# One kernel, five engine programs: the instruction order of attention, gated MLP and expert mixture written out as a table

## The chip, the core and the metric

The kernel runs on one core of a Trainium2 chip. A core has five engines with an instruction stream each: TensorE (PE in the profile; PEld is its loading of weights), VectorE (DVE), ScalarE (ACT), GpSimd (POOL) and SyncE (SP), which here only issues DMA transfers. Engines run beside each other and wait on semaphores for one another; within a stream, instructions start in the order in which they stand there. The metric is the device time of one execution in microseconds (us), as the median of several runs.

## The reference

Three stages, one after the other:

```python
# attention, 4 batches x 8 heads, 576 tokens, 64 wide; 32 landmarks = means of 18 tokens
A, Bm, C = sm(q, k_lm), sm(q_lm, k_lm), sm(q_lm, k)
Z = Bm.T / (norm1(Bm) * norminf(Bm) + 1e-6)
for _ in range(6): Z = 2 * Z - Z @ Bm @ Z
x = A @ Z @ C @ v                                   # -> 2304 tokens x 512
# gated MLP, 512 -> 1536 -> 512
xn = x / sqrt(mean(x * x) + 1e-6) * rms_g
x = (silu(xn @ w_gate) * (xn @ w_val)) @ w_out
# mixture: tokens with x @ w_skip > 0 add gate * relu(x @ w1[e]) @ w2[e], e = argmax(x @ w_gate2)
```

The three MLP weights arrive as 64-bit floats and are turned into 32-bit ones on the chip, by shifts and scaled copies on their bit patterns.

## The kernel before, in words

**Stages.** Attention works per batch in two groups of four heads (`group`): landmarks of k and q, three score matrices, then the iterated inverse (`inverse`). Its result is not formed in full: per batch a small matrix `WT` remains, and `products` multiplies it into the weights (P = WT x weight, kept as a high and a low half, `rsplit`). The MLP then runs in eight units of 288 tokens (`run_unit`): for each of 12 blocks `gemm` gives `pg` and `pv`, ACT takes a tanh of `pg` (tile `h`) and casts the product to `h_t`, POOL subtracts to get the low half, and `project` sums over all 12 blocks into `o`, which goes to `x2T`. `finish` stores x2T, makes the logits (`lp`) and transposes x2T for the output. Two calls of `mixture` follow, and a loop for more expert/batch pairs.

**Weights.** `load_raw` loads a piece of w_gate or w_val (256 rows by 512 columns of 64-bit floats, 1 MB, tile `wr`, three buffers that it shares with q and k of batch 0); `convert_w` turns it into tile `wo` by four operations (DVE scales into `s64`, ACT makes two partial copies into `wo`, DVE combines) and stores it to a scratch tensor in HBM (`wg_d`, `wv_d`) for later batches. Twelve pieces are treated so, five of them beside the attention of batch 0 and the rest during unit 0. `load_wout` and `convert_wout` do the same for twelve pieces of w_out.

**What sets the order.** The program is emitted once, in Python; generators in the list `side` are advanced between the matmuls of the main line by `slot()`, which goes by rough sums of busy time that `Paced` keeps per engine (`PER`, `FIXED`, `SLACK`). The framework's scheduler then orders each engine's stream from the emission order and its dependencies. Every operation of PE, DVE, ACT and POOL goes through `Paced.__getattr__`, so all of them carry line L62 in the profile. SP's transfers keep their own lines: L230 loads q and k, L254 v, L771 raw gate/value weights, L781 stores converted ones, L789 loads w_out, L812 loads converted weights again, L949 stores results, L1255 loads the scale `gcol`.

In the rows, `plm` are the landmark sums, `pb`, `sq`, `sk` scores, `nr`/`nu` the matmuls of the inverse, `X` and `Rb` its running matrices, `blk` its last X spread on a block diagonal, `pG`, `Gbd` and `oT` what follows, `asum`, `arec`, `sT`, `AT` the softmax of the first score matrix and its transposition.

Of the kernel before, what the change touches and what calls it, by code (L numbers as in the profile page):

```python
# [35 lines left out]
NC0 = 5  # L36
SLACK = 700


class Paced:  # L40

# [3 lines left out]

    def __init__(self, eng, busy, name):
        self.eng, self.busy, self.name = eng, busy, name

    def __getattr__(self, op):
        f = getattr(self.eng, op)  # L50

        def call(*args, **kw):
            size = max(math.prod(a.shape[1:]) for a in args[:3] if hasattr(a, "shape"))
            if self.name == "P":
                a = args[1] if op == "transpose" else args[2]
                size = math.prod(a.shape[1:])
                if op == "matmul" and a.dtype == F32:
                    size *= 4
                    if args[1].shape[0] == D:
                        size /= 2  # L60
            self.busy[self.name] += self.FIXED[self.name] + size * self.PER[self.name]
            return f(*args, **kw)  # L62

        return call


def attention_moe_kernel(
    tc, q, k, v, w_gate, w_val, w_out, rms_g, w_skip, w_gate2, w1, w2, out
):
    nc = tc.nc  # L70
    busy = dict.fromkeys("VAGP", 0.0)
    V, A, G, PE = (
        Paced(e, busy, n)
        for e, n in (
            (nc.vector, "V"), (nc.scalar, "A"), (nc.gpsimd, "G"), (nc.tensor, "P")
        )
    )
    SP = nc.sync
    ctx = ExitStack()

    def pool(stack, name, bufs=1, **kw):
        return stack.enter_context(tc.tile_pool(name=name, bufs=bufs, **kw))
# [36 lines left out]
    at = pool(pha, "at", side="right")  # L119
# [93 lines left out]
    def wo_tile(dt):  # L213
        return big.tile([128, 2, DM], dt, name="wo", tag="wo", bufs=FC)
# [10 lines left out]
    def load_qk(b, hg, n, t=None):  # L225
        if t is None:
            t = raw.tile([128, J, D], F32, name="kq")
        else:
            t = t.rearrange("p (j d) -> p j d", d=D)
        SP.dma_start(  # L230
            t.rearrange("p j d -> p (j d)"),
# [13 lines left out]
    def load_v(b, h0):  # L245
# [7 lines left out]
        for t in range(3):  # L253
            SP.dma_start(  # L254
                vt[32 * t : 32 * t + 32].rearrange("l h c d -> l h (c d)"), vv[t]
# [505 lines left out]
    def parts_at(d, i):  # L761
        n, g, q = PARTS[i]
        w = d.shape[1] // NQ
        return d[256 * g : 256 * g + 256, w * q : w * q + w].rearrange(
            "(c p) n -> p c n", p=128
        )

    def load_raw(i):
        if i < len(PARTS) and i not in raws:
            r = st1.tile([128, 2, J * D], I32, name="wr", tag="raw")[:, :, 0 : 2 * DM]  # L770
            SP.dma_start(r, parts_at(wsrc[PARTS[i][0]].bitcast(I32), i))  # L771
            raws[i] = r.rearrange("p c (n t) -> p c n t", t=2)

    def convert_w(i):
# [4 lines left out]
        for a in (1, 2):  # L779
            load_raw(i + a)  # L780
        SP.dma_start(parts_at(w_d[PARTS[i][0]], i), w)  # L781
        wparts[PARTS[i]] = w
# [3 lines left out]
    def load_wout(f):  # L786

        r = wo_tile(I32).rearrange("p a n -> p (a n)")
        SP.dma_start(r, w_out.bitcast(I32)[128 * f : 128 * f + 128, :])  # L789
        wo_raw.append(r.rearrange("p (n t) -> p n t", t=2))  # L790
# [9 lines left out]
    def load_w(n, q, last=False):  # L800

        ws = []
        for c in range(2):
# [7 lines left out]
            for g in range(2):  # L811
                SP.dma_start(  # L812
                    w[64 * g : 64 * g + 64],
# [221 lines left out]
    def ld(lst, idx, mx):  # L1035
        return nc.values_load(
            lst[0:1, bass.ds(idx, 1)], engines=(SPE,), min_val=0, max_val=mx
        )

    def number(lst):  # L1040
        return nc.values_load(lst[0:1, 2 * LP : 2 * LP + 1], min_val=0, max_val=B * E)

    def pair_at(lst, i):
        return ld(lst, i, E - 1), ld(lst, i + LP, B - 1)
# [166 lines left out]
    def drain(g):  # L1211
        for _ in g:
            pass
        if g in side:
            side.remove(g)
# [3 lines left out]
    def run_unit(u, before):  # L1219
# [32 lines left out]
        fin.append(finish(u, x2T))  # L1252
        side.insert(0, fin[0])

    SP.dma_start(gcol, rms_g.rearrange("(g c p) -> p g c", p=128, g=2))  # L1255

    def first_convs():
# [136 lines left out]
    for _ in mixture(*first["pair"], after_first, False):  # L1394
        next(oth, None)
        next(oth, None)
    drain(mixture(*second[0], lambda: pair_at(rest[0], 1), True, rest[1]))
    npairs = number(rest[0])
    with tc.For_i(0, npairs) as i:
        e, b = pair_at(rest[0], i + 1)  # L1400
# [36 lines left out]
```

## Time and profile before

| | |
|---|---|
| median of 3 runs | 673.87 us (672.52 to 674.31) |
| profiled execution, its own time | 678.17 us |
| span of its instructions | 676.4 us |
| busy: PE, DVE, ACT, POOL | 632.3, 434.9, 275.8, 146.4 us |
| instructions: PE, DVE, ACT, POOL | 4963, 997, 593, 162 |
| HBM read, written | 76.97 MB, 19.34 MB |

The span is the time from the first to the last instruction; 1.77 us of the profiled execution lie around it. PE is busy for 93% of the span, but not evenly: the busy tenths in 40 slices of 16.9 us begin 5, 7, 6, 7, 9, 8, 8 and stand at 9 nearly throughout after the tenth slice. The same part of the line PEclk (the granted clock of TensorE in tenths of full speed) reads 8, 9, 7, 7, 8, 8, 8. So the first 130 us are the part in which PE waits and runs below full speed. A time beside a matmul is what it took in its place; at a lower granted clock the same matmul takes longer.

### The profile page before, as it was taken

The page shows a single profiled execution, that of the slowest core. Times are in us where ns is not written, and L with a number is a line of the kernel's source. Part 1 is how long each engine was busy: PE and PEld are TensorE (multiplying, and loading weights), DVE is VectorE, ACT ScalarE, POOL GpSimd, SP SyncE. Part 2 cuts the span into 40 slices and gives each one's busy share as a digit, 9 for nine tenths or more (in the row PEclk, how much of TensorE's full clock was granted, in tenths as well). Part 3 has the DMA queues.
Part 4 walks back from the last instruction along what each step waited for, and adds up shares of the span by engine and source line. Part 5 has one row for each costly group of instructions (what it writes and reads, how often), then busy time and mean ns, then how long its engine had stood idle before and what let it go on. Part 6 is the DMA issues. An engine that isn't in the chain of part 4 may idle for free.

```text
span 676.4 us, 13386 instructions
## 1 busy us (share of the span) xinstructions
PE 632.3 (93%) x4963; PEld 548.9 (81%) x4963; DVE 434.9 (64%) x997; ACT 275.8 (41%) x593; POOL 146.4 (22%) x162
## 2 busy tenths in 40 slices
PE   5767988889998999999999999999999999999997
PEld 5653558877976888979889978999999988988985
DVE  6877778779769678896759966451645354353351
ACT  2358878534125422432531444240533343243240
POOL 5000234214101400410320320140552033033030
PEclk8977888999999999999999999999999999999999
DMA  8557779443248444249453316501644564364463
GB/s 274 216 215 251 261 264 336 117 107 87 71 104 215 93 110 106 67 126 194 87 110 87 75 45 147 126 8 27 178 127 100 165 206 140 123 174 146 141 181 137
DMA packets 111566, 97.16 MB, mean 144 GB/s; under 512 B 50192, under 2 KB 92176, under 8 KB 111504
## 3 DMA queue, kind: packets, MB, share of 16 engines
q1 hardware_dynamic: 111504, 96.34, 50.5%
q8 instruction: 38, 0.62, 0.4%
q14 instruction: 24, 0.20, 0.1%
HBM read 76.97 MB, written 19.34 MB: 142 GB/s over the span
## 4 chain that ended last, share of the span: by engine, by line
PE 74%; DVE 12%; DMA 6%; ACT 4%; issue 2%; POOL 1%; SPq 1%; POOLq 0%; DVEq 0%; ACTq 0%
PE o L62 18%; PE py L62 12%; PE ph L62 11%; PE pv L62 10%; PE pg L62 8%; PE P L62 4%; PE sq L62 3%; DMA wo<-in_moe_w_out_dram 2%; PE nr L62 2%; DMA wr<-wv_d 2%; DMA kq<-in_q_dram 2%; ACT wo L62 1%; DVE h L62 1%; DVE P L62 1%; PE sk L62 1%
## 5 line engine op out<-in xcount | busy, mean ns | idle before, releaser
L62 PE MATMUL o<-h_t,wo 128*128 128x288 f32 x1152 | 166.4, 300 | 3.6 <-ACT wo L62 1.8
L62 PEld LDWEIGHTS o<-h_t,wo 128*128 128x128 f32 x1152 | 156.0, 190 | 10.9 <-issue 5.1
L62 POOL TENSOR_TENSOR h_t<-h,h_t 128x288 fp32r<-128x288 f32 x96 | 83.8, 875 | 340.6 <-ACT h_t L62 274.7
L62 PE MATMUL pg<-ap_t,P 128*128 128x288 f32 x576 | 99.6, 303 | 7.9 <-DVE h L62 3.1
L62 PE MATMUL pv<-ap_t,P 128*128 128x288 f32 x576 | 99.5, 302 | 3.2 <-DVE P L62 1.6
L62 PEld LDWEIGHTS pg<-ap_t,P 128*128 128x128 f32 x576 | 82.8, 189 | 21.3 <-issue 9.3
L62 PEld LDWEIGHTS pv<-ap_t,P 128*128 128x128 f32 x576 | 83.0, 189 | 8.9 <-issue 2.7
L62 PE MATMUL ph<-xsh,P 128*128 128x288 f32 x384 | 77.6, 295 | 0.0
L62 PEld LDWEIGHTS ph<-xsh,P 128*128 128x128 f32 x384 | 61.9, 188 | 0.3
L62 DVE SCALAR_TENSOR_TENSOR h<-h,pg 128x288 f32<-128x288 f32 x96 | 42.6, 447 | 28.6 <-ACT h L62 28.1
L62 ACT CAST h_t<-h 128x288 fp32r<-128x288 f32 x96 | 41.1, 430 | 41.5 <-DVE h L62 41.4
L62 PE MATMUL ph<-xsl,P 128*128 128x288 f32 x192 | 56.8, 296 | 0.0
L62 ACT ACTIVATE h<-pg 128x288 f32<-128x288 f32 x96 | 39.2, 409 | 42.5 <-PE pg L62 37.9
L62 PE MATMUL py<-wo,h_t 128*128 128x512 f32 x210 | 51.4, 395 | 0.0
L62 PEld LDWEIGHTS py<-wo,h_t 128*128 128x128 f32 x210 | 39.4, 188 | 9.6
L62 DVE TENSOR_TENSOR h<-h,pv 128x288 f32<-128x288 f32 x96 | 42.8, 450 | 5.9 <-PE pv L62 1.8
L62 DVE STREAM_TRANSPOSE T<-kq 64x576 f32<-64x576 f32 (+1 forms) x40 | 35.4, 886 | 5.9 <-DMA kq<-in_k_dram 4.1
L62 ACT CAST P<-P 128x512 fp32r<-128x512 f32 x48 | 26.1, 586 | 31.2 <-PE P L62 30.6
L62 DVE TENSOR_TENSOR P<-P,P 128x512 fp32r<-128x512 f32 x48 | 31.4, 684 | 9.3 <-ACT P L62 9.2
L62 POOL TENSOR_TENSOR P<-w1r,P 128x512 fp32r<-128x512 f32 x16 | 21.0, 1315 | 72.3 <-ACT P L62 72.2
L62 PEld LDWEIGHTS ph<-xsl,P 128*128 128x128 f32 x192 | 36.0, 188 | 0.1
L62 DVE SCALAR_TENSOR_TENSOR h_t<-ph,h_t 128x288 fp32r<-128x288 f32 (+2 forms) x45 | 14.6, 353 | 27.6 <-ACT h_t L62 27.6
(222 smaller groups left out, 864.2 us busy)
## 6 DMA issues: line engine op xcount, KB each, us to landing
wl<-wg_d SPq DMA_DIRECT2D x36, 256.0 KB, 4.7
wr<-wv_d SPq DMA_DIRECT2D x32, 256.0 KB, 5.4
w1r<-in_moe_w_dram SPq DMA_DIRECT2D x32, 256.0 KB, 3.2
wr<-in_moe_w_gate_dram SPq DMA_DIRECT2D x6, 1024.0 KB, 6.7
wr<-in_moe_w_val_dram SPq DMA_DIRECT2D x6, 1024.0 KB, 6.6
wo<-in_moe_w_out_dram SPq DMA_DIRECT2D x12, 512.0 KB, 6.6
wo<-in_moe_w_dram SPq DMA_DIRECT2D x24, 256.0 KB, 5.1
kq<-in_k_dram SPq DMA_DIRECT2D x8, 576.0 KB, 4.1
```

The lines of the kernel that those rows point to most:

```text
L62: return f(*args, **kw)
```

## The change

A table `ORDER` is added: five lists, for PE, DVE, ACT, POOL and SP, each of pairs (skip, count) that walk through the instructions of that engine in the order in which they were emitted and so name a new order. `Paced` records every instruction it emits in `traced`, and a class `Queue` does so for SP's transfers. `arrange()`, called once behind the second mixture and before the loop, ties each instruction of an engine to the one that the table puts ahead of it, by an edge that only fixes their order. Nothing is computed otherwise: the instructions on each engine are the same ones, in the same number, on the same tiles. The table's order was found by list scheduling with durations taken from traces.

```diff
+ORDER = [
+    [int(x) for x in s.split()]
+    for s in (
+        "0 9 2 9 -11 2 9 4 4 5 -8 3 -4 1 8 4 2 5 -7 1 6 16 -22 1 21 7 4 1 -4 3 -4 1 4 3 1 "
...
+    )
+]
@@ class Paced
+        self.traced = []
...
         def call(*args, **kw):
+            ins = f(*args, **kw)
+            self.traced.append(ins.ins)
...
-            return f(*args, **kw)
+            return ins
@@
+class Queue:
+    def __init__(self, eng):
+        self.eng, self.traced = eng, []
+
+    def dma_start(self, *args, **kw):
+        ins = self.eng.dma_start(*args, **kw)
+        self.traced.append(ins.ins)
+        return ins
@@ def attention_moe_kernel
-    SP = nc.sync
+    SP = Queue(nc.sync)
@@
+    def arrange():
+        info = mybir.DependencyInfo(
+            mybir.DependencyClass.NoSync, mybir.DependencyReason.DATA
+        )
+        for eng, runs in zip((PE, V, A, G, SP), ORDER):
+            at, last = 0, None
+            for skip, n in zip(runs[0::2], runs[1::2]):
+                at += skip
+                for ins in eng.traced[at : at + n]:
+                    if last is not None:
+                        tc.add_manual_dep(ins, last.name, info, reason="order")
+                    last = ins
+                at += n
@@
     drain(mixture(*second[0], lambda: pair_at(rest[0], 1), True, rest[1]))
+    arrange()
```

In the changed kernel the recorded operations carry L160 and SP's transfers L183.

**The start.** On PE, before, the landmark sums of the second group (`plm_200`) stand on both sides of the small score matmul `pb`:

```order
L62 MATMUL plm_166<-kq_138,ident_94 128x128 x9
L62 MATMUL plm_200<-kq_141,ident_94 128x128 x5
L62 MATMUL pb_192<-lmk0_165,bdq_190 128x32 x2
L62 MATMUL plm_200<-kq_141,ident_94 128x128 x4
L62 MATMUL sq_215<-T_162,bdq_190 128x288 x2
```

and now:

```order
L160 MATMUL plm_166<-kq_138,ident_94 128x128 x9
L160 MATMUL plm_200<-kq_141,ident_94 128x128 x9
L160 MATMUL pb_192<-lmk0_165,bdq_190 128x32 x2
L160 MATMUL sq_215<-T_162,bdq_190 128x288 x2
L160 MATMUL sq_218<-T_162,bdq_190 128x288 x2
```

The last four of the second group's sums have moved ahead of `pb`, and the scores `sq` follow it at once. On SP the load of `gcol` has moved from the first place to the thirteenth, behind q, k and the first weights.

**The end of batch 0's attention.** On DVE, before, from the fourth step of the second group's inverse to the matrices that follow it (`s64` and `wo` are weight conversions):

```order
L62 TENSOR_TENSOR X_567<-nu_563,X_532 128x32
L62 SCALAR_TENSOR_TENSOR wo_311<-s64_312,wo_311 128x1024
L62 TENSOR_REDUCE asum_520<-sT_505 128x18
L62 TENSOR_TENSOR X_575<-nu_571,X_567 128x32
L62 TENSOR_SCALAR asum_520<-asum_520 128x18
L62 RECIPROCAL arec_523<-asum_520 128x18
L62 TENSOR_TENSOR X_583<-nu_579,X_575 128x32
L62 TENSOR_TENSOR sT_505<-sT_505,arec_523 128x576
L62 TENSOR_SCALAR s64_346<-wr_275 128x1024
L62 STREAM_TRANSPOSE AT_133<-sT_505 128x576
L62 TENSOR_TENSOR X_587<-nu_585,X_583 128x32
L62 TENSOR_TENSOR blk_589<-X_587,mask_105 128x128
```

and now:

```order
L160 TENSOR_TENSOR X_567<-nu_563,X_532 128x32
L160 SCALAR_TENSOR_TENSOR wo_311<-s64_312,wo_311 128x1024
L160 TENSOR_TENSOR X_575<-nu_571,X_567 128x32
L160 RECIPROCAL crec_465<-csum_463 128x1
L160 TENSOR_SCALAR mrn_295<-mask_105,rn_289 128x4
L160 TENSOR_SCALAR mrn_495<-mask_105,rn_489 128x4
L160 TENSOR_TENSOR X_583<-nu_579,X_575 128x32
L160 TENSOR_TENSOR X_587<-nu_585,X_583 128x32
L160 TENSOR_TENSOR blk_589<-X_587,mask_105 128x128
L160 TENSOR_SCALAR s64_346<-wr_275 128x1024
L160 TENSOR_TENSOR Gbd_594<-pG_591,mrn_295 128x256
L160 TENSOR_REDUCE asum_520<-sT_505 128x18
```

The softmax sum, its division, the transposition to `AT` and one conversion have left the place between `X_567` and `blk_589`; they stand behind `blk_589` now, and three small operations have come in.

**Unit 0.** On ACT, before, the partial copies of weight conversions (`wo`) alternate with the unit's own work (`h` the tanh, `h_t` its cast, `P0`, `P1` casts of products):

```order
L62 ACT_TABLE_LOAD
L62 ACTIVATE h_727<-pg_720 128x288
L62 ACTIVATE h_747<-pg_740 128x288
L62 ACTIVATE wo_818<-wr_776 128x1024
L62 CAST h_t_679<-h_727 128x288
L62 ACTIVATE wo_847<-wr_815 128x1024
L62 CAST h_t_679<-h_747 128x288
L62 ACTIVATE h_767<-pg_760 128x288
L62 ACTIVATE wo_847<-wr_815 128x1024
L62 ACTIVATE h_796<-pg_789 128x288
```

and now:

```order
L160 ACT_TABLE_LOAD
L160 ACTIVATE h_727<-pg_720 128x288
L160 ACTIVATE h_747<-pg_740 128x288
L160 ACTIVATE wo_847<-wr_815 128x1024 x2
L160 CAST P1_675<-P_827 128x512
L160 ACTIVATE wo_896<-wr_824 128x1024 x2
L160 ACTIVATE wo_945<-wr_853 128x1024 x2
L160 CAST h_t_679<-h_727 128x288
L160 ACTIVATE h_767<-pg_760 128x288
```

Six partial copies now stand between the second and the third tanh, and the cast of the first block has moved behind them. On SP, before, each load of a raw weight stands behind a store of a converted one:

```order
L771 DMA wr_776<-in_moe_w_val_dram 128x2x1024
L781 DMA wg_d_58<-wo_770 128x2x512
L771 DMA wr_815<-in_moe_w_gate_dram 128x2x1024
L781 DMA wv_d_59<-wo_809 128x2x512
L771 DMA wr_824<-in_moe_w_gate_dram 128x2x1024
L781 DMA wv_d_59<-wo_818 128x2x512
L771 DMA wr_853<-in_moe_w_val_dram 128x2x1024
L781 DMA wg_d_58<-wo_847 128x2x512
```

and now:

```order
L183 DMA wr_776<-in_moe_w_val_dram 128x2x1024
L183 DMA wg_d_58<-wo_391 128x2x512
L183 DMA wr_815<-in_moe_w_gate_dram 128x2x1024
L183 DMA wg_d_58<-wo_770 128x2x512
L183 DMA wr_824<-in_moe_w_gate_dram 128x2x1024
L183 DMA wv_d_59<-wo_809 128x2x512
L183 DMA wr_853<-in_moe_w_val_dram 128x2x1024
L183 DMA wv_d_59<-wo_818 128x2x512
```

Every load has moved ahead of one store: `wr_815` stood behind the store of `wo_770` and now stands before it, and so for the next ones.

Further on, the transposition of a unit's result for the output (`x2`) has moved from between the two DVE evacuations of `o` to some 20 places behind them, later products stand earlier in the `o` matmuls at the end of a unit, and loads of converted weights stand ahead of result stores on SP. In the two mixtures PE's order is unchanged.

## Rows read from the trace of the kernel before

**Rows 1.** Busy time by stage: window, us, busy (count) per engine, PEclk, DMA share, GB/s.

```profile
0.00:59.00 59.00, 40.12 (x272) 31.97 (x272) 41.67 (x131) 27.41 (x52) 8.64 (x26) 0.86 0.66 230
59.00:104.80 45.80, 40.52 (x198) 24.72 (x199) 36.89 (x62) 36.66 (x61) 11.17 (x10) 0.89 0.80 281
104.80:132.00 27.20, 22.34 (x150) 21.11 (x148) 22.36 (x36) 20.18 (x35) 10.62 (x9) 0.94 0.68 206
132.00:213.00 81.00, 74.31 (x642) 62.75 (x643) 64.26 (x149) 27.48 (x69) 12.20 (x14) 1.00 0.45 113
213.00:500.00 287.00, 283.47 (x2651) 253.34 (x2652) 194.14 (x472) 107.96 (x267) 69.98 (x80) 1.00 0.44 104
500.00:676.40 176.40, 171.57 (x1057) 155.03 (x1056) 75.60 (x151) 56.13 (x111) 33.76 (x25) 1.00 0.49 149
```

**Rows 2.** PE at the start: start us, us, engine, line, operation, tiles [idle before].

```profile
13.02 0.74 PE L62 MATMUL pb<-lmk,bdq 128*128 128x32 f32 x4 [1.91 <-DVE bdq L62]
13.57 2.06 PE L62 MATMUL plm<-kq,ident 128*128 128x128 f32 x8
15.42 1.17 PE L62 MATMUL sq<-T,bdq 128*128 128x288 f32 x2
```

**Rows 3.** SP at the start: the issue of the first load.

```profile
0.80 0.45 SPq L1255 DMA_DIRECT2D gcol<-in_moe_rms_g_dram  x1
```

**Rows 4.** DVE at the end of batch 0's attention.

```profile
41.48 0.19 DVE L62 TENSOR_TENSOR X<-nu,X 128x32 f32<-128x32 f32 x1 [1.30 <-PE nu L62]
41.76 1.23 DVE L62 SCALAR_TENSOR_TENSOR wo<-s,wo 128x1024 int32<-128x1024 int32 x1
42.90 0.75 DVE L62 TENSOR_REDUCE asum<-sT 128x18 f32<-128x576 f32 x1
43.56 0.18 DVE L62 TENSOR_TENSOR X<-nu,X 128x32 f32<-128x32 f32 x1
...
44.47 0.19 DVE L62 TENSOR_TENSOR X<-nu,X 128x32 f32<-128x32 f32 x1 [0.32 <-PE nu L62]
44.58 0.75 DVE L62 TENSOR_TENSOR sT<-sT,arec 128x576 f32<-128x576 f32 x1
45.24 0.69 DVE L62 TENSOR_SCALAR s<-wr 128x1024 f32<-128x1024 f32 x1
45.85 0.77 DVE L62 STREAM_TRANSPOSE AT<-sT 128x576 f32<-128x576 f32 x1
...
46.73 0.29 DVE L62 TENSOR_TENSOR blk<-X,mask 128x128 f32<-128x128 f32 x1
```

**Rows 5.** ACT in the same stretch: two partial copies of a conversion.

```profile
43.58 2.52 ACT L62 ACTIVATE wo<-wr 128x1024 int32<-128x1024 uint16 x2
```

**Rows 6.** SP's longest waits on stores of converted weights: total, times, longest us.

```profile
SPq L781 <- DVE wo L62: 48.7, 8, 17.7
```

**Rows 7.** From the chain of waits, unit 0: start us, us, what.

```profile
101.36 11.65 DMA wo<-in_moe_w_out_dram
```

**Rows 8.** PE, first matmuls of unit 1.

```profile
131.95 1.07 PE L62 MATMUL pg<-ap_t,P 128*128 128x288 f32 x6 [1.59 <-DVE x2T L62]
```

**Rows 9.** DVE in the w_out conversions: one operation twice.

```profile
107.68 1.57 DVE L62 TENSOR_TENSOR wo<-wf,wo 128x512 fp32r<-128x512 f32 x1 [1.54 <-ACT wo L62]
...
112.64 0.69 DVE L62 TENSOR_TENSOR wo<-wf,wo 128x512 fp32r<-128x512 f32 x1
```

**Rows 10.** POOL beside the first of the two.

```profile
107.44 1.26 POOL L62 TENSOR_TENSOR wo<-wf,wo 128x512 fp32r<-128x512 f32 x1
```

**Rows 11.** Busy time by window at the end of batch 0's attention, columns as above.

```profile
40.00:60.00 20.00, 13.01 (x52) 9.39 (x52) 12.39 (x25) 13.92 (x22) 0.00 (x0) 0.66 0.80 263
```

**Rows 12.** PE: products of WT and a weight, in two places.

```profile
61.59 3.42 PE L62 MATMUL P<-wo,WT 128*64 128x512 f32 x8
...
78.21 1.93 PE L62 MATMUL P<-wo,WT 128*64 128x512 f32 x6
```

99 rows, old and new, of the table ORDER are left out of this document.

## The prediction

> **What bounds the kernel now.** I read the profile from coarse to fine. First the table of busy time by stage [rows 1]. There the reader is to compare PE's busy time with the length of each stretch, and to read the granted clock beside it. From 213 us on PE is busy for 283.47 of 287.00 us and 171.57 of 176.40 us at a clock of 1.00: 3.5 and 4.8 us of idle in 463 us. Up to 213 us it is idle for 59.00 - 40.12 = 18.9, 45.80 - 40.52 = 5.3, 27.20 - 22.34 = 4.9 and 81.00 - 74.31 = 6.7 us, 35.8 us in all, and the clock stands at 0.86, 0.89 and 0.94 in the first three. So whatever an order can win is won before 213 us; behind it PE's own work is the bound and a new order has next to nothing to fill. Second, the timelines of PE, DVE and ACT at the two places where PE stands before a named operation [rows 2, 4]. Third, the waits of SP's queue and the chain of waits in unit 0 [rows 6, 7], which tell whether weights or engines come last.
>
> The profiled execution took 678.17 us for a span of 676.4. The sum is made against it; it lies 4.30 us above the median of 673.87, and I carry the difference over unchanged.
>
> **A, the start.** Between `pb` and the first `sq` stand eight records of `plm` (four matmuls of two passes), and `sq` begins 15.42 - 13.57 = 1.85 us after them [rows 2]. The change puts them ahead of `pb`, where PE idled 1.91 us for DVE's `bdq`; their tile was already being read by the sums ahead of that wait, so they fit in. The chain through `sq` gets 1.85 us shorter. The load of `gcol` leaves the head of SP's queue, which is worth at most its issue of 0.45 us [rows 3], and only if k and q land earlier by it. Bounds 0 to -2.3; I take **-1.8**. What hides the moved matmuls is the wait for `bdq`; if DVE gets there sooner too, part of the 1.85 comes back as PE's own work.
>
> **B, the end of batch 0's attention.** DVE runs the last steps of the second inverse: `X_567` at 41.48, `blk` at 46.73 [rows 4]. Between them stand the sum 0.75, the division 0.75, a conversion 0.69 and the transposition 0.77, together 2.96 us, that no step of the inverse needs. Without them the chain is: the combine of `wo_311` ends at 41.76 + 1.23 = 42.99, then `X_575`, and each further step takes one turn over PE, 44.47 - 43.56 = 0.91 (at 44.47 DVE had waited for PE, so this is a true turn). Two turns put `X_587` at 44.81 and `blk` at 45.00 instead of 46.73: -1.7. The three small operations that come in lie inside a turn. The four that leave are run behind `blk`: 0.75 + 0.75 + 0.77 = 2.27 us of them lie ahead of `AT`, which PE needs for the second group's `oT` only; what hides them is the work of the first group. Without that cover they cost 2.27 and the step is worth +0.5; if all 2.96 us are won it is -3.0. I take **-1.7**.
>
> **C, unit 0, 59 to 132 us.** PE is idle here for 10.1 of 73 us. DVE is busy for 36.89 + 22.36 = 59.25 us, idle for 13.7; ACT for 56.84, idle for 16.2 [rows 1]. Neither is full, and yet PE waits: the three engines wait for one another and for weights in turn. Stores of converted weights hold SP's queue, waiting for DVE's combine, for 48.7 us in eight waits, the longest 17.7 [rows 6], and until now each raw load was queued behind such a store. The table puts each load one store earlier, and takes ACT's copies in runs, so that a combine is ready whenever DVE comes free. I take half of DVE's idle time as won, 6.9 us. Against it stands one cost that the order shows: ACT now runs six copies between the second and the third tanh, before two. Four more at 2.52 / 2 = 1.26 us [rows 5] are 5.0 us; behind them wait the third tanh, DVE's product with it, POOL's split, and PE for the bank of the sum `pg`. PE's cover is a product of WT and weights, eight records in 3.42 us [rows 12]; 1.6 us stay. So -6.9 + 1.6 = **-5.3**. PE's floor is -10.1; upwards 0, unless the rival below holds. These are the widest ends in the sum, and I take about the middle because both causes (queue and turns) can be seen and no row tells which is last.
>
> DVE's subtraction that makes a low half took 1.57 us at 107.68 with a POOL subtraction beside it from 107.44 to 108.70, and 0.69 us at 112.64 with none [rows 9, 10]. The Trainium skill says in "SBUF — State Buffer", section "Who interferes with whom", that a DVE instruction with two SBUF inputs contends with a GpSimd instruction that reads SBUF; the trace agrees with 0.88 us for one meeting. By that rule, packing the two engines closer would take back up to 0.88 us for each such meeting; with 12 pieces of w_out that is an estimate of some 10 us at worst, half of them on POOL's side, and would leave C near zero.
>
> **D, 132 to 213 us.** The first matmul of unit 1 waits 1.59 us for DVE's evacuation of `x2T` [rows 8], between whose two halves a transposition of 128x576 stood, 0.77 us in its shape [rows 4]. It is moved some 20 places back: -0.8. Of the other 5.1 us of idle I give a quarter to products and loads that stand earlier: -1.2. **-2.0**, bounds -6.7 (no idle left) and +1.6 (one more such wait).
>
> **E, 213 to 500 us.** Idle 3.5 us; the same transposition at later unit ends is hidden for the most part. **-0.5**, bounds -3.5 and +1.6. **Rest:** PE's order is unchanged in the mixtures, idle 4.8 us: **0**, within 1.0 either way.
>
> Sum: -1.8 - 1.7 - 5.3 - 2.0 - 0.5 = -11.3. The profiled execution would take 666.9 us, the median 673.87 - 11.3 = **662.6 us**.
>
> **The rivals.**
>
> *1. ACT starves TensorE and its clock stays low (slower).* At the end of attention, 40 to 60 us, PE was busy for 13.01 of 20.00 us and the granted clock was 0.66 [rows 11]. The same product took 3.42 / 8 = 0.43 us a record at 61.59 and 1.93 / 6 = 0.32 us at 78.21, where the clock had risen [rows 12]. If the run of copies on ACT leaves PE such gaps, the 40.52 us of PE's work from 59 to 104.8 us, done at a mean of 0.89, need 40.52 x 0.89 / 0.66 = 54.6 us, 8.8 more than the 45.80 of that stretch. C is then +8.8, and the whole -6.0 + 8.8 = +2.8: 676.7 us. It makes the kernel slower by more than 0.3% from C = +8.0 on, which is 53.8 us for this work: a mean clock there below 40.52 x 0.89 / 53.8 = 0.67. For it: the six copies. Against it: the attention ends sooner, and PE has products to run. The Trainium skill, "TensorE: Matmul & The Clock Gate", section on the clock gate, has the slow clock as the resting state, which activity releases; by that rule this rival and the fourth are two sides of one thing.
>
> *2. The transfers come last.* The DMA share is 0.80 and 0.68 in unit 0, and the chain goes 11.65 us through loads of w_out from 101.36 us [rows 1, 7]. If the loads only queue elsewhere, C lies between 0 and -2.0; with -1.0 the total is -7.0: 666.9 us. For it: that piece, and 281 GB/s, the highest rate of any stretch [rows 1]. Against it: the stores that hold SP's queue wait for DVE and not for a transfer [rows 6].
>
> *3. Turns, not order.* If each engine's new order only moves the waits between PE, DVE and ACT, A alone is left: 672.1 us, no change.
>
> *4. PE's floor.* With weights always there, PE's idle time goes: A -2.3, B -1.7, C -10.1, D -4.0, E -2.0, together -20.1: 653.8 us. For it: 35.8 us of idle ahead of 213 us, of which this takes half. Against it: DVE is at 81% in unit 0 already.
>
> That the change does not do what it says is excluded: the rows of all five engines differ.
>
> **How the numbers follow.** Forecast (-11.3) 0.50; transfers 0.20; PE's floor 0.12; turns 0.10; ACT and the clock 0.08. What a measurement of this kernel can tell from no change is about 0.3%, 2.0 us: faster is below 671.9, slower above 675.9. Faster: 0.50 + 0.20 + 0.12 = 0.82. Same: 0.09, rival 3 less a hundredth for its upper end. Slower: 0.08 + 0.01 = 0.09. The range leaves out the first rival and what of the floor goes beyond 20 us: 651 to 673.
>
> **What would show it.** A: `sq` begins near 13.6 us in the changed trace. B: `blk` follows `X_567` by 3.5 us instead of 5.25, beside what A moved. C: PE's idle time in unit 0 near 5 us, and SP's waits on stores of converted weights much shorter; a clock below 0.8 there speaks for rival 1, a DMA piece as long as before in the chain for rival 2. D: no wait of 1.6 us before unit 1's first `pg`. The prediction is wrong if the stretch from 213 us on moves by more than 2 us, or if the first 132 us give back less than 5.

## The result and the profile after

The changed kernel took 665.12 us in the median of 4 runs (664.48 to 669.46), the one before 674.09 (672.52 to 675.18): -9.0 us, a ratio of 0.9885 (95% interval 0.9845 to 0.9925). Measured again with other runs of the kernel before it was 666.46 against 674.78, 0.9862 (0.9829 to 0.9896). The forecast was -11.3 us. Its profiled execution took 669.46 us with a span of 667.6, the slowest of its four; the two profiled executions differ by 8.7 us, about as the medians do.

First the busy time by stage of the changed kernel, columns as in [rows 1]:

```profile
0.00:59.00 59.00, 44.38 (x288) 34.69 (x288) 45.93 (x136) 30.14 (x57) 8.51 (x26) 0.86 0.83 268
59.00:104.80 45.80, 38.32 (x204) 26.77 (x202) 35.11 (x62) 38.36 (x63) 11.26 (x11) 0.89 0.91 317
104.80:132.00 27.20, 22.05 (x150) 20.19 (x150) 21.47 (x34) 16.83 (x31) 9.07 (x7) 1.00 0.38 99
132.00:213.00 81.00, 78.08 (x680) 65.12 (x681) 66.55 (x158) 29.09 (x74) 14.22 (x17) 0.98 0.45 108
213.00:500.00 287.00, 284.07 (x2654) 256.13 (x2653) 193.38 (x463) 105.51 (x261) 68.41 (x78) 1.00 0.45 104
500.00:667.60 167.60, 163.07 (x993) 146.52 (x991) 73.81 (x148) 55.61 (x110) 32.99 (x24) 0.99 0.50 152
```

Length less PE's busy time gives its idle time: 14.6, 7.5, 5.2, 2.9, 2.9 and 4.5 us, where [rows 1] give 18.9, 5.3, 4.9, 6.7, 3.5 and 4.8. The attention and the stretch from 132 to 213 us have gained. From 59 to 132 us PE is idle for 2.5 us more, where the forecast wanted 5 less.

Fixed windows hold different work once everything has moved, so the second view follows single instructions: the start (in one row the end) of the same instruction in both traces, changed less before, in us. A unit's first four blocks use the product P0, the next four P1, so its fifth block has the first matmul with P1.

| instruction | at (before) | changed less before | gained since the line above |
|---|---|---|---|
| DVE, reciprocal of the norm (`rbs`), end of the attention | 59.14 | -5.41 | -5.4 |
| PE, end of the last sum `o` of unit 0 | 130.36 | -4.24 | +1.2 |
| PE, first `pg` of unit 1 | 131.95 | -5.99 | -1.8 |
| PE, first `pg` with the product P1 in unit 1, its fifth block | 143.38 | -2.98 | +3.0 |
| PE, start of the last sum `o` of unit 7 | 509.45 | -8.50 | -5.5 |
| end of the span | 676.4 | -8.8 | -0.3 |

So the gain is made twice and 2.4 us of it are lost between, from the reciprocal to the fifth block of unit 1. That loss has two parts. Up to the end of unit 0's sums PE is idle for 11.3 us instead of 8.4. Behind them it is idle for 2.68 us in both kernels, but its matmuls take 1.3 us longer. Four places show how.

The start, on PE of the changed kernel, where [rows 2] had `plm` between `pb` and `sq`:

```profile
8.77 2.79 PE L160 MATMUL plm<-kq,ident 128*128 128x128 f32 x18
12.22 0.63 PE L160 MATMUL pb<-lmk,bdq 128*128 128x32 f32 x4 [0.66 <-DVE bdq L160]
12.69 2.19 PE L160 MATMUL sq<-T,bdq 128*128 128x288 f32 x8
```

`sq` starts at 12.69, 2.73 us earlier than before; the wait for `bdq` has shrunk from 1.91 to 0.66 us, filled by the moved sums.

The last steps of the inverse, on DVE, answering to [rows 4]:

```profile
39.74 0.19 DVE L160 TENSOR_TENSOR X<-nu,X 128x32 f32<-128x32 f32 x1 [1.05 <-PE nu L160]
39.85 1.21 DVE L160 SCALAR_TENSOR_TENSOR wo<-s,wo 128x1024 int32<-128x1024 int32 x1
40.98 0.18 DVE L160 TENSOR_TENSOR X<-nu,X 128x32 f32<-128x32 f32 x1
...
41.90 0.19 DVE L160 TENSOR_TENSOR X<-nu,X 128x32 f32<-128x32 f32 x1 [0.40 <-PE nu L160]
42.88 0.19 DVE L160 TENSOR_TENSOR X<-nu,X 128x32 f32<-128x32 f32 x1 [0.79 <-PE nu L160]
43.10 0.29 DVE L160 TENSOR_TENSOR blk<-X,mask 128x128 f32<-128x128 f32 x1
```

`blk` follows the first of these X by 3.36 us, before by 5.25; each turn over PE takes 0.92 and 0.98 us.

Unit 0, on ACT: the copies of weight conversions that the table takes in one run, and the cast and the tanh that stand behind them:

```profile
70.96 2.54 ACT L160 ACTIVATE wo<-wr 128x1024 int32<-128x1024 uint16 x2
73.46 0.59 ACT L160 CAST P<-P 128x512 fp32r<-128x512 f32 x1
73.94 4.99 ACT L160 ACTIVATE wo<-wr 128x1024 int32<-128x1024 uint16 x4
78.80 0.40 ACT L160 CAST h_t<-h 128x288 fp32r<-128x288 f32 x1
79.11 0.40 ACT L160 ACTIVATE h<-pg 128x288 f32<-128x288 f32 x1
```

The same at the start of the unit, copies ahead of the casts that the first `pg` needs:

```profile
58.99 2.54 ACT L160 ACTIVATE wo<-wr 128x1024 int32<-128x1024 uint16 x2
...
62.37 1.07 ACT L160 CAST P<-P 128x512 fp32r<-128x512 f32 x2 [0.24 <-issue]
```

And PE's waits in the same unit, with the first of them as it was before in a fence of its own:

```profile
63.10 0.50 PE L160 MATMUL pg<-ap_t,P 128*128 128x288 f32 x2 [3.73 <-ACT P L160]
...
80.60 0.80 PE L160 MATMUL pg<-ap_t,P 128*128 128x288 f32 x4 [1.74 <-DVE h L160]
```

```profile
66.60 0.51 PE L62 MATMUL pg<-ap_t,P 128*128 128x288 f32 x2 [1.59 <-ACT P L62]
```

ACT is busy nearly all the time ahead of those waits, with work that nobody waits for yet. PE waits 3.73 us (before: 1.59) for the cast of the first product, and 1.74 us for a block whose tanh stands behind 4.99 us of copies. The weights do come earlier: SP's waits for converted weights fall to

```profile
SPq L183 <- DVE wo L160: 39.3, 9, 21.5
```

from 48.7 us [rows 6], and the loads of w_out begin at 80.68 instead of 89.92. The piece of 11.65 us of w_out loads in the chain [rows 7] is gone. But earlier weights did not make unit 0 shorter.

The wait of 1.59 us ahead of unit 1 [rows 8] has left its place and come back, longer, at the third block:

```profile
124.77 1.35 PE L160 MATMUL o<-h_t,wo 128*128 128x288 f32 x9
125.96 0.96 PE L160 MATMUL pg<-ap_t,P 128*128 128x288 f32 x6
...
132.23 1.23 PE L160 MATMUL pg<-ap_t,P 128*128 128x288 f32 x6 [2.68 <-DVE h L160]
```

Before, PE waited 1.59 us here and 1.09 us some blocks later; now it waits the same 2.68 us in one piece. DVE's product `h`, for which it waits, stands behind the transposition of batch 1's q, and that waits 2.45 us for its load. SP issues this load as soon as DVE has transposed k, in both kernels (before at 129.00 us, the transposition done at 128.98; now at 124.80 and 124.71), and the chain of waits goes through it in both, first before, then now:

```profile
129.00 5.32 DMA kq<-in_q_dram
```

```profile
124.80 5.64 DMA kq<-in_q_dram
```

After the long wait the granted clock was 0.64 for some microseconds (before, it was 1.00 from 132 to 143.4 us), and PE's matmuls took longer:

```profile
132.30:137.00 4.70, 4.70 (x41) 4.14 (x42) 3.80 (x12) 0.73 (x2) 1.01 (x1) 0.64 0.41 127
```

### The profile page after: what moved, and what is told of

Read it like the earlier page. It is cut to its first block, busy times and chain, and to the rows that moved or that the text cites. A ratio compares the mean times of both kernels' runs of the same rounds, so it can differ in the third digit from the quotient of the medians.

```text
span 667.6 us, 13388 instructions
## 1 busy us (share of the span) xinstructions
PE 630.0 (94%) x4963; PEld 549.4 (82%) x4963; DVE 436.3 (65%) x997; ACT 275.5 (41%) x593; POOL 144.5 (22%) x162
## 4 chain that ended last, share of the span: by engine, by line
PE 74%; DVE 5%; ACT 4%; DMA 2%; issue 2%; POOL 1%; SPq 1%; POOLq 0%; ACTq 0%
PE o L160 19%; PE py L160 12%; PE ph L160 12%; PE pv L160 10%; PE pg L160 10%; PE P L160 4%; PE sq L160 2%; ACT wo L160 1%; PE sk L160 1%; PE nr L160 1%; PE lp L160 1%; DMA kq<-in_q_dram 1%; ACT wf L160 1%; DMA wr<-wv_d 1%; POOL wo L160 1%
## 5 line engine op out<-in xcount | busy, mean ns | idle before, releaser
L160 PE MATMUL o<-h_t,wo 128*128 128x288 f32 x1152 | 164.8, 299 | 3.5 <-POOL wo L160 1.6
L160 PEld LDWEIGHTS o<-h_t,wo 128*128 128x128 f32 x1152 | 154.5, 188 | 11.0 <-issue 4.8
L160 POOL TENSOR_TENSOR h_t<-h,h_t 128x288 fp32r<-128x288 f32 x96 | 82.3, 860 | 338.0 <-ACT h_t L160 318.2
L160 PE MATMUL pg<-ap_t,P 128*128 128x288 f32 x576 | 99.9, 306 | 10.4 <-DVE h L160 6.6
L160 PEld LDWEIGHTS pg<-ap_t,P 128*128 128x128 f32 x576 | 83.5, 192 | 22.0 <-issue 11.1
L160 PE MATMUL pv<-ap_t,P 128*128 128x288 f32 x576 | 98.5, 304 | 0.7 <-ACT P L160 0.4
L160 PEld LDWEIGHTS pv<-ap_t,P 128*128 128x128 f32 x576 | 84.1, 192 | 5.4 <-issue 1.9
L160 PE MATMUL ph<-xsh,P 128*128 128x288 f32 x384 | 77.6, 295 | 0.0
L160 ACT ACTIVATE h<-pg 128x288 f32<-128x288 f32 x96 | 39.4, 411 | 70.9 <-PE pg L160 65.8
L160 DVE SCALAR_TENSOR_TENSOR h<-h,pg 128x288 f32<-128x288 f32 x96 | 42.7, 447 | 30.0 <-ACT h L160 29.5
L160 PEld LDWEIGHTS ph<-xsh,P 128*128 128x128 f32 x384 | 61.9, 188 | 0.3
L160 PE MATMUL ph<-xsl,P 128*128 128x288 f32 x192 | 56.9, 296 | 0.0
L160 PE MATMUL py<-wo,h_t 128*128 128x512 f32 x210 | 51.4, 395 | 0.0
L160 DVE TENSOR_TENSOR h<-h,pv 128x288 f32<-128x288 f32 x96 | 43.0, 449 | 10.1 <-PE pv L160 4.8
L160 PEld LDWEIGHTS py<-wo,h_t 128*128 128x128 f32 x210 | 39.4, 188 | 9.6
L160 ACT CAST h_t<-h 128x288 fp32r<-128x288 f32 x96 | 41.0, 429 | 14.5 <-DVE h L160 13.9
L160 ACT CAST P<-P 128x512 fp32r<-128x512 f32 x48 | 27.0, 589 | 31.8 <-PE P L160 31.1
L160 DVE STREAM_TRANSPOSE T<-kq 64x576 f32<-64x576 f32 (+1 forms) x40 | 35.5, 887 | 6.2 <-DMA kq<-in_q_dram 2.9
L160 DVE TENSOR_TENSOR P<-P,P 128x512 fp32r<-128x512 f32 x48 | 32.1, 683 | 11.2 <-ACT P L160 10.9
L160 POOL TENSOR_TENSOR P<-w1r,P 128x512 fp32r<-128x512 f32 x16 | 20.7, 1294 | 72.2 <-ACT P L160 71.7
L160 PEld LDWEIGHTS ph<-xsl,P 128*128 128x128 f32 x192 | 36.0, 188 | 0.1
L160 DVE SCALAR_TENSOR_TENSOR h_t<-ph,h_t 128x288 fp32r<-128x288 f32 (+2 forms) x45 | 14.6, 353 | 27.6 <-ACT h_t L160 27.6
```

Of the source, the lines that this page charges most:

```text
L160: ins = f(*args, **kw)
```

## The experiments

Each kernel was timed beside the kernel before on the same chip. In all of them nothing but order is changed. In the diffs `row` is an engine's list of instructions in the table's order, and CHAIN stands for the loop that ties `row` together. A move (a, n, b) takes n instructions from a on and puts them behind b.

**e1 and e2: the table in two halves.**

```diff
-            row (whole)
+            row = row[: names.index(CUT[name])]     # e1: up to the end of batch 0's attention
+            row = row[names.index(CUT[name]) :]     # e2: from there on
```

> The table's order only up to the end of batch 0's attention (about 57 us); all behind it is ordered as before. In the changed kernel's trace, the instructions there come 5.4 us earlier (the reciprocal of the norm) and the first matmul of unit 0 3.5 us earlier. Theory 1 (each stretch keeps what it wins): 3.5 to 5 us faster than before, 669 to 670.5. Theory 2 (unit 0's end waits for weights of w_out and their conversion, whatever is won ahead of it): at the first matmul of unit 1 less than 1.5 us of it is left, 672.5 to 674.

> The complement: the order as before up to the end of batch 0's attention, the table's order from unit 0 on. Theory 1: 4 to 5.5 us faster than before, 668.5 to 670, most of it at the ends of units behind 200 us, and nothing won between 60 and 130 us. Theory 2: the whole gain of the change is made by the earlier loads and conversions of unit 0, so this alone gives 7 us or more, under 667.

e1 took 671.17 us, ratio 0.9952 (0.9928 to 0.9975), -3.2 us; e2 671.68 us, 0.9957 (0.9935 to 0.998), -2.7 us. So each half gives about a third of the whole, and neither theory 2 holds: e1's lead of 4.6 us at the reciprocal is 6.0 us at the end of unit 0's sums and 6.8 us at the P1 matmul of unit 1 (unit 0 ordered as before keeps it), and e2 does not have the whole gain. e1 came out a little under its 3.5 to 5, e2 under its 4 to 5.5. In e2's trace the table's unit 0 shows the same two waits in another execution, and by the last block of its sums it has lost 2.5 us against the reciprocal ahead of it:

```profile
65.17 0.50 PE L163 MATMUL pg<-ap_t,P 128*128 128x288 f32 x2 [2.36 <-ACT P L163]
...
82.54 0.81 PE L163 MATMUL pg<-ap_t,P 128*128 128x288 f32 x4 [1.74 <-DVE h L163]
```

**e3, e4 and e8: unit 0's table with ACT's work put forward.**

```diff
+    "A": [("I-738", 1, "I-851"), ("I-768", 1, "I-830"), ...],     # e3: casts and tanh
+    "V": [("I-769", 2, "I-831"), ("I-798", 1, "I-786"), ...],     # ahead of pieces 6 and 7
+    "A": [("I-812", 2, "I-688"), ("I-821", 2, "I-698")],          # e4: copies behind casts
+    "V": [("I-814", 1, "I-689")],                                 # (e8: e3's and e4's, and more)
```

> The table with one edit: in unit 0 the casts of the first two blocks and the third and fourth tanh on ACT, and their products on DVE, stand ahead of the conversions of the sixth and seventh weight pieces that the table put before them. Theory 1 (PE's idle time at 79 to 82 us, 1.7 + 0.4 us and more, comes from these copies and is kept to the end): 1.5 to 3 us faster than the changed kernel, 662 to 663.5. Theory 2 (the sums at the end of unit 0 wait for converted weights, and the conversions come later now): the wait at 80 us goes, but the first matmul of unit 1 starts as before or up to 2 us later; 665 to 667.

> The table with another edit: at the start of unit 0 the casts of the first products P0 and of the activations on ACT stand ahead of the copies of two weight conversions (four copies of 1.2 us), and the same on DVE. Theory 1: PE's wait of 3.7 us before the first matmul of unit 0 shrinks by 2 us or more, and 1.5 to 2.5 us of it stay to the end, 662.5 to 663.5. Theory 2: the conversions behind are late by what is won here, and the time is that of the changed kernel, 664.5 to 666.

> The edits of e3 and e4 together, and the casts of the second and third product P1 on ACT and DVE ahead of the sixth weight piece too, where e3's trace has a new wait of 1.9 us at 77 us. Theory 1 (waits on ACT in the first half of unit 0 cost PE time that is kept to the end): 2.5 to 4 us faster than the changed kernel, 661.5 to 663. Theory 2 (the sums o at the end of unit 0 wait for the conversions that are now later): e3's gain is all there is or less, 663.5 to 666.

e3 took 663.91 us, 0.9866 (0.9832 to 0.9901); e4 666.26, 0.9881 (0.9852 to 0.9909); e8 666.53, 0.9869 (0.9836 to 0.9902). None can be told from the changed kernel. e3's median lies 0.4 us above theory 1's range. Its trace loses nothing in unit 0: from the reciprocal to the end of unit 0's sums it is 2.2 us shorter than before, where the changed kernel is 1.2 longer. But the intervals overlap, so that is not settled. e4 and e8 refute theory 1 as it was put, and their traces show why. In e4 the first wait falls, and the later one grows:

```profile
59.03 0.50 PE L166 MATMUL pg<-ap_t,P 128*128 128x288 f32 x2 [1.71 <-ACT P L166]
...
78.99 1.33 PE L166 MATMUL pg<-ap_t,P 128*128 128x288 f32 x4 [4.50 <-DVE h L166]
```

In e8 ACT itself stands still, since the conversions that free the load buffers are later and the next copy waits for its weights at the head of the queue, with a cast behind it for which PE waits 3.76 us:

```profile
81.23 1.12 ACT L175 ACTIVATE wo<-wr 128x1024 int32<-128x1024 uint16 x1 [2.12 <-DMA wr<-in_moe_w_val_dram]
82.25 0.58 ACT L175 CAST P<-P 128x512 fp32r<-128x512 f32 x1
```

A wait taken out of a full in-order queue came back at its next place. e4 and e8 lie 0.3 and 0.5 us above theory 2's ranges, so its reading, that nothing is won, holds for both; the place that it named in e8, the sums at the end of unit 0, is not where the wait came back.

**e5 and e6: unit 0 ordered as before between two pieces of the table.**

```diff
+            a, b = names.index(CUT[name]), names.index(CUT2[name])
+            for part in (row[:a], row[b:]):
+                CHAIN
```

> The changed kernel once more, as the base for the three beside it: 665 to 666.5.

> The table up to the end of batch 0's attention and again from unit 1 on; unit 0 between them (conversions, loads of w_out, products, sums) ordered as before. Theory 1 (from the traces of e1 to e4: against the last step ahead of it, the table's unit 0 ends 1.2 to 2.5 us later than the one ordered as before ends, which won 1.4 us): the table's unit 0 is a loss of 2.5 to 4 us, and this kernel is 2 to 3.5 us faster than the changed one, 662 to 663.5. Theory 2 (unit 0 in the table's order loads w_out 10 us earlier and that pays in unit 1): 666 to 668.

e5, the base, took 666.46 us; e6 663.11, 0.9814 (0.9782 to 0.9845). On the same chip that is 3.35 us faster than the changed kernel with theory 1's size, and the lowest median measured here; the two intervals against before overlap by a little (0.9829 to 0.9896 for e5). The traces agree. From the reciprocal to the P1 matmul of unit 1, a stretch with the same work in all, the changed kernel takes 2.4 us more than before and e6 2.1 us less. The lines are the changed kernel, e5, e6 and before:

```profile
53.73:140.40 86.67, 72.70 (x429) 56.67 (x430) 66.15 (x116) 59.24 (x102) 22.90 (x21) 0.90 0.68 224
50.85:137.46 86.61, 72.94 (x428) 56.96 (x429) 66.67 (x116) 59.28 (x102) 22.67 (x21) 0.90 0.68 226
52.63:134.73 82.10, 71.42 (x429) 54.95 (x429) 66.40 (x116) 59.44 (x102) 23.17 (x21) 0.94 0.71 235
59.14:143.38 84.24, 73.15 (x428) 54.97 (x429) 67.81 (x116) 59.62 (x102) 24.33 (x21) 0.92 0.74 241
```

Of the 4.5 us between e5 and e6, 3.0 are idle time of PE (13.7 against 10.7 us) and 1.5 are slower matmuls at the lower clock. The clock is also higher in all runs of e6 (0.984 to 0.990 over the whole run) than in those of e5 (0.977 to 0.983). How much of that follows from the shorter waits was not tested, so the 3.35 us are not all waits.

**e7 and e10: SP's list alone taken out, or kept alone in unit 0.**

```diff
+            if name == "S": continue                                   # e7
-            for part in (row[:a], row[b:]):                            # e10, on e6
+            for part in (row[:a], row[b:]) if name != "S" else (row,):
```

> The table on PE, DVE, ACT and POOL, and SP's transfers left to the scheduler. Theory 1 (compute queues make the gain; in unit 0 loads are ahead of need by 10 us and more): within 1.5 us of the changed kernel. Theory 2 (each load one store earlier makes the gain): half of the gain or more is lost, 669 to 672.

> As e6, but SP's transfers in the table's order throughout, unit 0 included: raw weights and w_out are issued there up to 10 us earlier while PE, DVE, ACT and POOL run unit 0 as before. Theory 1 (in unit 0 the engines wait for ACT's and DVE's queues, not for weights): within 1 us of e6, 662 to 664. Theory 2 (the prediction's cause in its step C, that loads queued behind stores): 2 us or more faster than e6, under 661.

e7 took 671.82 us, 0.9945 (0.9921 to 0.9969): theory 2, 5.4 us slower than the changed kernel beside it, so more than half of the gain hangs on the order of transfers. But not where theory 2 had it. At the end of unit 0's sums e7 stands at -3.8 us against before, the changed kernel at -4.2; behind it, from the P1 matmul of unit 1 to the last sum of unit 7, e7 gains nothing (+0.3 us) where the changed kernel gains 5.5. The two later stages of e7, and what PE waits for there:

```profile
132.00:213.00 81.00, 77.25 (x711) 63.94 (x709) 67.36 (x159) 29.69 (x75) 14.45 (x17) 1.00 0.49 120
213.00:500.00 287.00, 281.28 (x2601) 253.15 (x2594) 191.95 (x459) 104.54 (x260) 68.59 (x77) 0.99 0.42 100
```

```profile
PE P L162 <- DMA wr<-wv_d: 3.4, 2, 2.3
```

PE's order has the products of a later batch earlier; without SP's list their weights are still queued behind result stores (four loads of `wr` that the changed kernel issues from 220.29 us on, ahead of eight stores, come behind those stores in e7, from 234.92 us on), and PE's idle time from 213 to 500 us is 5.7 us, more than the 3.5 of before. In unit 0 it is the other way round: e10, which issues the first load of w_out at 80.33 us (e6: 83.89) and the third at 81.72 (e6: 89.28), took 663.30 us, 0.9839 (0.979 to 0.9888), the same as e6. That is theory 1: unit 0, in the order of before on the other engines, does not wait for weights.

**e9: the table from unit 1 on alone.**

```diff
+            row = row[names.index(CUT2[name]) :]
```

> The table's order only from unit 1 on; attention of batch 0 and unit 0 as before. In the traces PE's idle time from 130 to 500 us is 11.8 us before and 5.4 to 7.9 in the changed kernel. Theory 1 (the stretches add up: 3.2 us from the attention, a loss of about 3 in unit 0, the rest from unit 1 on): 5 to 8 us faster than before, 666.5 to 669.5. Theory 2 (the later part only pays because the earlier stretches are early): less than 3 us faster, 671.5 or more.

669.09 us against 673.38, 0.9924 (0.9892 to 0.9955): 4.3 us faster by the medians, 5.1 by the ratio, theory 1 at its lower end. From the P1 matmul of unit 1 to the last sum of unit 7 its trace gains 5.3 us, as the changed kernel's does (5.5). The ratios of e1 and e9 multiply to 0.9952 x 0.9924 = 0.9876; e6, which has both parts, was at 0.9814. That is more than the two together, by slightly more than their intervals explain; e10, which has both parts too, was at 0.9839, within them. This was not followed up.

**e11 and e12: the wait at the end of unit 0, on e6 and e10.**

```diff
+    "V": [("I-1361", 1, "I-1307")],                                       # e11: evacuation of o
+          ("I-1712", 1, "I-1363"), ("I-1720", 1, "I-1712")                # e12, beside it
```

> As e6, with one operation moved: DVE's first evacuation of o at the end of unit 0 stands behind the first of the landmark sums of batch 1 and not behind all of them. In e6's trace PE waits 1.57 us for that evacuation ahead of unit 1. Theory 1 (the wait at the end of unit 0 comes from the landmark work ahead of the evacuation on DVE, not from the transposition behind it): the wait goes, 1 to 1.6 us faster than e6, 661.5 to 662.5. Theory 2: the accumulator of the next matmul is freed by something else as late, and the time stays 662.5 to 664.

> As e10 (attention and everything from unit 1 on by the table, SP by the table throughout, unit 0 of the four other engines as before), with the evacuation moved as in e11 and, beside it, the first block's two products on DVE ahead of the transposition of q of batch 1. In e11's trace the wait of 1.6 us ahead of unit 1 was gone, and one of 1.66 us stood 5 us later, behind that transposition, which waits 1.4 us for the load of q. Theory 1 (the second wait is that of DVE's queue behind the load): both waits go, 1.5 to 2.5 us faster than e10, 661 to 662, a ratio to before of about 0.981. Theory 2 (PE waits for batch 1's scores or for the tanh anyway): a third wait takes its place, 663 to 664.

e11 took 664.91 us, 0.9857 (0.9812 to 0.9902), e12 664.06, 0.9855 (0.982 to 0.9891); neither is faster than e6 and e10. The wait went where it should; the first line is e10's PE, the second e11's, the third e12's:

```profile
123.19 1.06 PE L164 MATMUL pg<-ap_t,P 128*128 128x288 f32 x6 [1.59 <-DVE x2T L164]
```

```profile
125.75 1.07 PE L165 MATMUL pg<-ap_t,P 128*128 128x288 f32 x6 [1.66 <-DVE h L165]
```

```profile
129.44 1.06 PE L167 MATMUL pg<-ap_t,P 128*128 128x288 f32 x6 [1.15 <-DVE h L167]
```

Each time it comes back as a wait for DVE's product `h` of a later block; in e11 that stood behind the transposition of q, which waited 1.40 us for its load. For e12 theory 2 holds; in e11 theory 1 is right about the cause of the wait and wrong about the time. The evacuation was not what ended last there: the load of q, issued when k has been transposed, is not moved by it. In e11 the clock fell besides, behind the wait of 1.66 us. Three microseconds of e10, then of e11, PE busy throughout, with 41 records of matmuls and with 32:

```profile
127.00:130.00 3.00, 3.00 (x41) 2.69 (x41) 2.90 (x8) 0.73 (x2) 0.82 (x1) 1.00 0.65 197
```

```profile
127.00:130.00 3.00, 3.00 (x32) 2.72 (x27) 2.72 (x9) 0.58 (x2) 0.81 (x1) 0.50 0.42 160
```

## Why the prediction came out as it did

The direction was right, and the size within 2.3 us, the latter partly by luck: C brought next to nothing, and gains elsewhere beyond their forecast made up for about half of it.

**A and B** (-1.8 and -1.7): right in mechanism and a little small. `sq` came 2.73 us earlier instead of 1.8, and `gcol`'s place in SP's queue has a part in it: the first sums, at 5.71 us before, start 0.9 us earlier, of which its issue of 0.45 [rows 3] explains half, and `blk` followed its X by 3.36 us where 3.5 was forecast. Alone they gave -3.2 us in time (e1). In the traces the reciprocal came 5.4 us earlier; part of that is not theirs, because e2 and e9, which have the order of before there, reached it 3.3 and 1.8 us earlier than the execution of [rows 1].

**C** (-5.3) failed. The step that failed is "I take half of DVE's idle time as won". It read idle time of DVE and ACT as room to be packed, and took the loads behind stores as the cause. In its place the trace shows, counted from the reciprocal, +1.2 us at the end of unit 0's sums, -0.6 at unit 1's first matmul, where the wait ahead of it has gone, and +2.4 at the P1 matmul, behind the place where that wait comes back. The loads did come earlier, but e10 shows that unit 0 does not need them earlier. The cost that the prediction did name, ACT's copies ahead of what PE needs, acts at two places (2.1 us more before the first `pg`, 1.74 at 80.60) where 1.6 us were priced for one. The traces show that the copies set those waits: with the copies moved, the first is 1.71 us in e4 and the second is gone in e3. They also show other waits in their stead (4.50 us in e4, 1.87 in e3), and in time neither can be told from the changed kernel. Put back to the old order, the stretch was 3.35 us faster (e6 against e5); by the ratios to before, e6 and e10 are 3.2 and 1.6 us faster than e5, with intervals that overlap. This is the first rival in part. ACT did starve PE, but the clock from 59 to 104.8 us stayed at 0.89, as before, and not below the 0.67 that it needed. The clock fell later, at the head of unit 1, where the matmuls took 1.3 us longer.

The cost of DVE and POOL meeting, up to 0.88 us each, did not grow: DVE's four subtractions `wo<-wf,wo` took 4.3 us in all before and 4.4 in the changed kernel.

**D and E** (-2.0 and -0.5): counted from unit 1's first matmul to the last sum of unit 7 they came to -2.5 in the changed kernel's trace, the forecast's own sum, but as +3.0 in the first four blocks and -5.5 behind them. Without the table's unit 0 ahead of it the later part alone gives -4.3 to -5.1 in time (e9). D's named cause was wrong: DVE's rows of before, here around the wait, show that the transposition starts after the wait has ended (131.95), so it cannot have caused it:

```profile
130.84 0.23 DVE L62 TENSOR_TENSOR lmk<-s 128x64 f32<-128x64 f32 x1
131.10 0.42 DVE L62 TENSOR_TENSOR bdk<-lmk,maskj 128x256 f32<-128x256 f32 x1
131.45 0.45 DVE L62 TENSOR_SCALAR x2T<-o 128x288 f32<-128x288 f32 x1
132.00 0.78 DVE L62 STREAM_TRANSPOSE x<-x2T 128x576 f32<-128x576 f32 x1
```

What held the evacuation was batch 1's landmark sums ahead of it. e11 confirms that by taking them away, and that removing this wait alone wins nothing, since the load of q ends later. E took PE's idle time as all there was to win. Of the 5.5 us, 3.5 are idle time and 2.0 are PE's own busy time (356.94 and 354.92 us for the same 3279 matmul records, at a clock of 1.00 in both); why it shrank was not tested. What the later stages gained, e7 shows, hangs on loads of converted weights moved ahead of result stores; the products moved forward on PE go with them, and the transfers alone were not tried there. The prediction had both in sight only as an aside. One of its signs of being wrong was met here: from unit 3's start (259.51 us before) to the end the kernel gained 2.8 us, more than the 2 that it allowed behind 213 us. The other, less than 5 us given back by 132 us, lies at its edge: -4.2 at the end of unit 0's sums, -6.0 at the next matmul.

The second rival (transfers come last) is refuted for unit 0's weights and true in another form later: the load of q comes last at the head of unit 1, in both kernels, and the converted weights would have come last behind it, had SP's list not gone with the others. Why the wait of [rows 8] leaves its place in the changed kernel while it stays in e1, e6 and e10 was not settled: DVE's order at that point is the table's in e6 too, so it comes with unit 0's order.

## What to carry to other kernels

Idle time of two engines that wait for each other is no room to be packed; ask which instruction at the head of each in-order queue the bound engine needs next, and price every place where something now stands ahead of it. An order made for several engines is one piece: SP's list was worth 5 us beside the lists of the other engines, and nothing in unit 0, where they had the old order. A wait that leaves its place has to be looked for at the next ones, and with it the clock behind it. And a table that wins as a whole can hold a stretch that loses; cutting it into stretches and putting each back to the old order found 1.6 to 3.4 us here, while moving single instructions within the losing stretch found none that could be measured.

## What was not expected of the hardware

The same program runs its first 60 us at different granted clocks in different executions. Two executions of the changed kernel, two stretches of 10 us; first the one profiled with the result, then e5:

```profile
10.00:20.00 10.00, 7.37 (x36) 5.67 (x35) 8.17 (x24) 4.33 (x9) 3.02 (x5) 0.84 0.83 237
40.00:50.00 10.00, 8.77 (x29) 6.93 (x30) 7.83 (x19) 7.95 (x14) 0.00 (x0) 0.62 0.79 271
```

```profile
10.00:20.00 10.00, 7.79 (x42) 5.80 (x40) 9.22 (x29) 4.79 (x10) 3.10 (x5) 1.00 0.84 247
40.00:50.00 10.00, 7.71 (x39) 5.35 (x38) 8.81 (x16) 9.03 (x14) 0.00 (x0) 0.83 0.97 329
```

The clock has two levels, 1.2 and 2.4 GHz, 0.5 and 1.0 in these rows; a value between is a mixture. One order, and it reached the reciprocal at 53.73 us in the first and 50.85 in the second. Over whole runs time goes roughly with the mean clock: e9's twelve runs span 665.86 us at 0.985 to 673.25 us at 0.975. So a single profiled execution of this kernel does not settle differences in time below 1%. Nor does the length of one wait tell whether the clock falls behind it: at the head of unit 1 it fell after waits of PE of 2.68 us (changed kernel), 2.51 (e5) and 1.66 (e11), and stayed at 1.00 after one of 2.33 (e2).
